# A late query transpose one slot earlier and a weight load one cycle later, in a fused attention and feed-forward kernel

## The chip, the cores and the metric

The kernel runs on one core of a Trainium2 chip. The metric is the device time of one execution in microseconds (us), the median of several runs. Five engines work side by side and meet at semaphores: TensorE (PE; its weight loads are shown apart as PEld), VectorE (DVE), ScalarE (ACT), GpSimd (POOL) and SyncE (SP). Each takes its own instructions strictly in program order, so an instruction that waits holds up all that is queued behind it on the same engine.

## What is computed

```python
def _attn_ref(q, k, v, tau):            # batch 8, heads 8, sequence 576, head size 64
    scores = (1.0 / np.sqrt(q.shape[-1])) * np.matmul(q, k.transpose(0, 1, 3, 2))
    thresh = np.max(scores, axis=-1, keepdims=True) - tau
    scores = np.where(scores >= thresh, scores, -1000000000.0)
    scores = scores - np.max(scores, axis=-1, keepdims=True)
    attn = np.exp(scores)
    attn = attn / (np.sum(attn, axis=-1, keepdims=True) + 1e-09)
    return np.matmul(attn, v)

def _moe_ref(x, w_in, w_out):           # x: 4608 x 512, w_in: 512 x 2048, w_out: 2048 x 512
    h = x @ w_in
    g = h * np.clip(h + 3.0, 0.0, 6.0) / 6.0
    return g @ w_out
```

The attention output, with its heads side by side, is the x of the feed-forward part. Only scores within tau (0.02) of the row's maximum take part in a softmax row.

## The kernel before

**Slots.** The work on the scores is cut into 8 x 18 = 144 slots (the list `queue`, lines 180 to 187). A slot is one batch b, one half g of its heads (a "quad" of four heads, number 2b + g), one tile t of 128 query rows, and a pair i of heads; the order within a batch is (g, t) = (0,0), (0,1), (1,0), (1,1), then the rest tile t = 4, and then (0,2), (0,3), (1,2), (1,3), each twice. The rest tile holds query rows 512 to 575 of both quads of a batch at once. Batch 1 has slots 18 to 35: slots 22 and 23 are tile 0 and slots 24 and 25 tile 1 of quad 3, and slots 26 and 27 are the rest tile of quads 2 and 3.

**What a slot goes through.** `burst(n)` (L216) computes on TensorE the raw scores of slots n and n + 1 into PSUM. Even slots have one place there and odd slots another, so a burst writes over the scores of the two slots before, in steps: part of the even slot, part of the odd slot, and then the rest. `sm_max` (L230) on VectorE copies a slot's scores to SBUF and takes their row maxima, two instructions and two reads of the accumulator; `sm_bias` (L239) on GpSimd makes the threshold from them; `sm_mask` (L244) and `sm_exp` (L249) on ScalarE reject and exponentiate; `sm_recip` (L252) on VectorE inverts the sums; `sm_norm` (L257) on GpSimd normalises and rounds. The result is transposed, on TensorE for slots below 10 (L277, copied by VectorE in L278 and L279), otherwise by a DMA that SyncE issues (L268), and is later multiplied with v (`av`, L286, copied in L294). The feed-forward part runs in between: `mm1` and `mm2_part` (both through L309), a relu (ScalarE L327 in odd slots, VectorE L329 in even ones), a gate (VectorE L342) and an eviction of the output (L361).

**Order.** The order on each engine is that of the program; nothing is rescheduled. There are two loops. The first (line 477) takes slots 0 to 13 in cycles of two; in a cycle n it issues, in one place, the entries `issues[n]` and `issues[n + 1]`, between the maxima of slots n + 2 and n + 3 (only cycle 0 splits them). The second (line 529) takes slots 14 to 143 one by one. In slot n of it stand, in this order: the maxima of slot n + 1 (in odd slots below 21, those of slot n + 2 further down), the reciprocal of slot n - 1, an attention product with its copy, at most one item of the first product with its gate, an eviction that was left over, a part of the second product in odd slots, ScalarE's exponentials and masks, the list `jobs[n]`, the normalisation of slot n - 1, in even slots the burst for slots n + 2 and n + 3, and `issues[n]`. Slots 22, 23 and 24 have no item of the first product.

**Jobs.** Queries and keys are loaded in their natural layout (`load`, L86) and brought into the layout for the scores by block transposes of 32 x 32 on VectorE: `transpose_k` (L110) in two parts, and `transpose_q` (L96) in two pieces, query columns 0 to 255 and 256 to 575. Lines 414 to 426 say in which slot each of these stands. For batch 1 that is a table of its own: quad 2 has its last piece in slot 22 and quad 3 in slot 24. For the other batches, counted from the first slot of the batch before, the last pieces stand in slots 20 and 22.

**Weights.** `load_w_in(i)` (L136) loads a quarter of w_in, 512 KB, with a conversion to bf16, and `load_w_out(i)` (L140) a quarter of w_out. GpSimd issues both, in its own order of instructions, between its biases and normalisations. Lines 442 to 445 give their slots. Quarter 3 of w_in holds hidden columns 1536 to 2047, which the first product reaches with its seventh item, in slot 20.

**Relays.** In a burst, a no-operation on another engine (SyncE in the first loop, GpSimd in the second) waits for the step before, and the burst's last eight or so matmuls, those to the odd slot's last 128 columns, wait for it (lines 204 to 207).

## Time and profile before

| what | value |
|---|---|
| median of 3 runs | 501.76 us (500.86 to 816.31) |
| the profiled execution | 501.7 us, of which 499.9 us are the span of its instructions |
| busy in the span | PE 484.7, DVE 445.8, ACT 441.6, POOL 294.1 us |
| mean granted TensorE clock | 0.997 |
| maxima, DVE L230 | 288 at 750 ns, 205.0 us busy |
| query transposes, DVE L96 | 33, from 404 to 837 ns |
| scores, PE L216 | 2560 matmuls, 168.6 us busy |
| input weight loads, POOL L136 | 4 issues of 512 KB, 747 to 795 ns each on GpSimd, 5.5 to 13.0 us to landing |

Times in the profile count from the first instruction of the span. "Idle before" is the time that an engine stood still before an instruction, with the engine and line that ended it. Ends of matmuls are modelled. The granted clock is the share of full speed at which TensorE was allowed to run. A line such as `DVE s L230 x4` in the chain of waits names engine, written tile, source line and the number of records.

### The profile page before, as it was taken

How to read it: one execution, taken by the hardware profiler on the slowest of the kernel's cores; microseconds unless marked ns; L12 is line 12 of the kernel's file. 1: busy time of each engine (PE TensorE's matmuls, PEld its weight loads, DVE VectorE, ACT ScalarE, POOL GpSimd, SP SyncE). 2: the span in 40 equal slices, each digit the busy share in tenths (PEclk: the TensorE clock that was granted, in tenths of full speed). 3: DMA queues.
4: the chain of work that ended last, by engine and by line, in shares of the span. 5: the costliest groups of instructions: out<-in, count | busy, mean ns of one | idle time of the engine just before them, and what ended most of it. 6: DMA issues, size and time to landing. Idle time of an engine off the chain costs nothing.

```text
span 499.9 us, 17390 instructions
## 1 busy us (share of the span) xinstructions
PE 484.7 (97%) x6797; PEld 359.5 (72%) x6802; DVE 445.8 (89%) x1154; ACT 441.6 (88%) x949; POOL 294.1 (59%) x537
## 2 busy tenths in 40 slices
PE   8888998999999999999999999999999999999996
PEld 7766765777777776777777776777777776777474
DVE  6999986999999999999999999999999999887243
ACT  3999997999999999999999999999999999999231
POOL 3786784666666666666666666766666565554000
PEclk9999998999999999999999999999999999999999
DMA  7999998997999887997999997998999878766421
GB/s 207 150 252 178 148 181 141 180 163 117 178 178 217 130 186 149 227 158 151 156 209 181 152 168 146 220 176 147 160 187 207 151 129 130 134 123 134 92 65 42
DMA packets 192770, 79.98 MB, mean 160 GB/s; under 512 B 171184, under 2 KB 183984, under 8 KB 192688
## 3 DMA queue, kind: packets, MB, share of 16 engines
q1 hardware_dynamic: 175456, 55.34, 65.0%
q0 software_dynamic: 16896, 23.07, 23.9%
q8 instruction: 53, 0.87, 0.7%
q10 hardware_dynamic: 336, 0.46, 0.3%
q14 instruction: 29, 0.24, 0.2%
HBM read 36.70 MB, written 9.44 MB: 92 GB/s over the span
## 4 chain that ended last, share of the span: by engine, by line
PE 82%; DVE 7%; issue 1%; ACT 1%; DMA 0%; SPq 0%; DVEq 0%
PE ps L309 48%; PE ps L216 27%; PE ps L286 7%; DVE s L230 4%; DVE g L342 1%; ACT r L327 1%; DVE osb L361 1%; DMA out_dram<-osb 0%; DVE kT L110 0%; DVE r L329 0%; DVE xT L294 0%; DVE pR L279 0%; SPq L376 0%; DVE qT L96 0%; DVE rinv L252 0%
## 5 line engine op out<-in xcount | busy, mean ns | idle before, releaser
L230 DVE TENSOR_SCALAR_CACHE_REDUCE s<-ps 128x576 f32<-128x576 f32 x288 | 205.0, 750 | 17.9 <-PE ps L216 15.2
L257 POOL TENSOR_SCALAR pn<-s,rinv 128x576 bf16<-128x576 f32 x288 | 210.8, 745 | 14.9 <-issue 1.3
L244 ACT ACTIVATE s<-s,bias 128x576 f32<-128x576 f32 x288 | 205.7, 762 | 8.3 <-POOL bias L239 8.3
L249 ACT ACTIVATE s<-s 128x576 f32<-128x576 f32 x288 | 192.3, 671 | 0.0
L216 PE MATMUL ps<-kT,qT 32*128 32x128 f32 (+3 forms) x2560 | 168.6, 418 | 6.5 <-DVE s L230 4.0
L216 PEld LDWEIGHTS ps<-kT,qT 32*128 32x128 f32 (+1 forms) x2560 | 125.1, 175 | 50.9 <-DVE s L230 11.5
L309 PE MATMUL ps<-xT,w_in_sb 128*64 128x256 bf16 (+1 forms) x1936 | 133.4, 275 | 0.5 <-DVE xT L294 0.5
L309 PE MATMUL ps<-w_out_sb,g 128*64 128x512 bf16 (+1 forms) x1020 | 130.8, 379 | 0.2
L309 PEld LDWEIGHTS <-w_in_sb 128*64 128x64 bf16 (+1 forms) x1936 | 106.0, 109 | 10.9 <-issue 3.3
L239 POOL TENSOR_SCALAR bias<-m 128x2 f32<-128x2 f32 (+1 forms) x147 | 27.6, 188 | 140.1 <-DVE rinv L252 125.9
L342 DVE SCALAR_TENSOR_TENSOR g<-r,ps 128x512 bf16<-128x512 f32 x128 | 87.4, 684 | 12.2 <-ACT r L327 8.5
L309 PEld LDWEIGHTS <-g 128*64 128x64 bf16 (+1 forms) x1024 | 61.6, 109 | 47.9 <-issue 0.2
L327 ACT ACTIVATE r<-ps,three 128x512 f32<-128x512 f32 x81 | 55.2, 686 | 22.8 <-PE ps L309 21.8
L249 ACT ACTIVATION_READ_ACCUMULATOR s<-s 128x1 f32 x288 | 54.6, 190 | 0.0
L286 PEld LDWEIGHTS <-v 128*64 128x64 bf16 x960 | 41.4, 111 | 15.8 <-issue 3.8
L286 PE MATMUL ps<-pT,v 128*64 128x256 bf16 x640 | 45.4, 273 | 1.3 <-DVE s L230 1.2
L329 DVE TENSOR_SCALAR r<-ps 128x512 f32<-128x512 f32 x63 | 43.3, 688 | 0.7 <-PE ps L309 0.4
L119 POOL DMA_DIRECT2D v<-in_v_dram x64 | 36.9, 578 | 10.1 <-DVE kT L110 4.7
L361 DVE TENSOR_SCALAR osb<-ps 128x512 f32<-128x512 f32 x32 | 21.9, 684 | 9.0 <-DMA out_dram<-osb 6.3
L110 DVE STREAM_TRANSPOSE kT<-nk 128x320 f32<-128x320 f32 (+1 forms) x64 | 26.3, 452 | 0.8 <-DMA nk<-in_k_dram 0.8
L294 DVE CAST xT<-ps 128x256 bf16<-128x256 f32 x64 | 26.0, 406 | 0.4
L96 DVE STREAM_TRANSPOSE qT<-nq 128x640 f32<-128x640 f32 (+2 forms) x33 | 24.6, 749 | 1.5 <-DMA nq<-in_q_dram 1.5
(35 smaller groups left out, 170.8 us busy)
## 6 DMA issues: line engine op xcount, KB each, us to landing
out_dram<-osb SPq DMA_DIRECT2D x140, 64.0 KB, 2.6
nk<-in_k_dram POOLq DMA_DIRECT2D x12, 576.0 KB, 4.9
nq<-in_q_dram POOLq DMA_DIRECT2D x12, 576.0 KB, 5.1
v<-in_v_dram POOLq DMA_DIRECT2D x32, 80.0 KB, 4.3
v<-in_v_dram POOLq DMA_DIRECT2D x32, 64.0 KB, 3.4
w_in_sb<-in_moe_w_in_dram POOLq DMA_DIRECT2D x4, 512.0 KB, 7.7
w_out_sb<-in_moe_w_out_dram POOLq DMA_DIRECT2D x4, 512.0 KB, 9.1
pT<-pn SPq DMA_TRANSPOSE x120, 4.5
```

What stands on the lines that cost most here:

```text
L119: nc.gpsimd.dma_start(out=vsb[b % 2][32 * g:32 * g + 32].rearrange("p (hp a) c -> p a hp c", a=2)[:, a, :, c0 * D:(c0 + count) * D], in_=v ...
L216: mm = nc.tensor.matmul(ps_flat[rows, c0:c0 + w], qT[c:c + 32, j, q0:q0 + rows.stop - rows.start], kT[c:c + 32, j, k0:k0 + w], start=(j == ...
L230: nc.vector.tensor_scalar(out=sl.s[:, i, :], in0=ps_flat[:, c0:c0 + S], scalar1=1.0, scalar2=None, op0=Alu.mult, op1=Alu.max, accum_out=sl ...
L239: nc.gpsimd.tensor_scalar(out=sl.bias[:, of], in0=sl.m[:, of], scalar1=-scale, scalar2=tau, op0=Alu.mult, op1=Alu.add)
L244: nc.scalar.activation(out=s, in_=s, func=Act.Prelu, bias=sl.bias[:, i:i + 1], scale=scale, alpha=REJECT)
L249: nc.scalar.activation(out=s, in_=s, func=Act.Exp, accum_out=sl.rsum[:, i:i + 1])
L257: nc.gpsimd.tensor_scalar(out=pn[:, i, :], in0=sl.s[:, i, :], scalar1=sl.rinv[:, i:i + 1], scalar2=1.0, op0=Alu.mult, op1=Alu.mult)
L286: nc.tensor.matmul(pb[a * 64:(a + 1) * 64, :], vsb[b % 2][:, 2 * hp + a, u * D:(u + 1) * D], pT[:, block, cols], start=(c == 0), stop=(c = ...
L309: nc.tensor.matmul(out[c:c + w], lhsT[:, c:c + w], rhs, start=start, stop=stop)
L327: nc.scalar.activation(out=r, in_=hps, func=Act.Relu, bias=three[:])
L329: nc.vector.tensor_scalar(out=r, in0=hps, scalar1=3.0, scalar2=0.0, op0=Alu.add, op1=Alu.max)
L342: nc.vector.scalar_tensor_tensor(out=out, in0=r, scalar=6.0, in1=hps, op0=Alu.min, op1=Alu.mult)
```

## The change

```diff
-        when = (((4, 8, 10, 22), (12, 14, 18, 24)) if b == 1 else ((8, 10, 12, 20), (14, 16, 18, 22)))[g]
+        when = (((4, 8, 10, 22), (12, 14, 18, 23)) if b == 1 else ((8, 10, 12, 20), (14, 16, 18, 22)))[g]
...
-    for i, n in enumerate((0, 2, 2, 3)):
+    for i, n in enumerate((0, 2, 2, 4)):
         at(issues, n, lambda i=i: load_w_in(i))
```

The first edit moves one instruction: `transpose_q(3, 8, T)`, query columns 256 to 575 of quad 3, stands in the jobs of slot 23 and no longer in those of slot 24. The second moves one DMA issue: quarter 3 of w_in is issued in the cycle of slots 4 and 5, between quad 2's query load (on SyncE's queue) and the first quarter of w_out, and no longer in the cycle of slots 2 and 3. No instruction is added or removed.

## The prediction

> **What bounds the kernel now.** I read the page first, then the chain of waits, then the timelines of the single engines around slot 24 and around the weight loads, and last the table by stage for the granted clock. The page says that TensorE is busy 97% of the span and that its granted clock was at nine tenths or more in 39 of 40 slices:

> ```profile
> PEclk9999998999999999999999999999999999999999
> ```

> The one 8 is the seventh slice, about 75 to 87.5 us. The chain of waits (start, duration, what; in us) has a stretch there in which it leaves TensorE for VectorE:

> ```profile
> 77.21 1.34 DVE s L230 x4
> 78.55 0.07 DVE rinv L252
> 78.62 0.32 DVE xT L294
> 78.95 0.60 DVE osb L361
> 79.54 0.76 DVE qT L96
> 80.31 0.04 issue
> 80.35 3.40 PE ps L216 x53
> 83.75 3.15 PE ps L309 x24
> ```

> The reader is to see that the burst of scores (L216) starts when the query transpose (L96) ends. Counted back in program order, this is slot 24. Its VectorE work is the maxima of slot 25 (L230, four records), a reciprocal, the copy of an attention product, an output eviction, and then the job of slot 24, the transpose of quad 3's columns 256 to 575. Right behind it in the program stands the burst for slots 26 and 27, the first that reads those columns: slots 26 and 27 are the rest tile (t = 4, query column 512 on) of quads 2 and 3. TensorE's timeline shows the same from its side, with an ordinary burst above it:

> ```profile
> 72.64 0.48 PE L216 MATMUL ps<-kT,qT 32*128 32x128 f32 x2
> 73.30 2.22 PE L216 MATMUL ps<-kT,qT 32*128 32x128 f32 x30 [0.17 <-DVE s L230]
> ...
> 77.93 0.43 PE L216 MATMUL ps<-kT,qT 32*64 32x128 f32 x2
> ```

> In the ordinary burst the first matmuls run early, and the other 30 start when the second maximum of the odd slot has been read. In slot 24 quad 2's first matmuls run at 77.93, and then TensorE waits 2.00 us for the transpose. The answer on the granted clock by stage (stretch; length; busy PE, PEld, DVE, ACT, POOL; clock; DMA):

> ```profile
> 47.00:50.40 3.40, 2.35 (x68) 1.79 (x68) 3.03 (x13) 3.40 (x9) 1.97 (x5) 1.00 1.26 124
> ...
> 77.90:81.30 3.40, 1.40 (x38) 1.07 (x41) 2.40 (x6) 3.40 (x8) 3.23 (x6) 0.98 0.47 112
> ```

> TensorE was busy 1.40 of 3.40 us here. In steps of half a microsecond, the clock is 1.00 to 81.0, 0.69 in the next step, 0.50 from 81.5 to 84.5, 0.90 to 85.0, and then 1.00 again. Elsewhere the emptiest stretch of 3.4 us that I found still has 2.35 us busy (47.0 to 50.4), and its clock is full. So slot 24 costs a wait and then about 3.3 us at half clock, the only such dip of the run. From 108 us on the chain is almost TensorE alone, so what is won at 80 us should arrive at the end.

> **Part 1, the transpose in slot 23.** Nothing is added or removed: one STREAM_TRANSPOSE of 128x640 (0.83 us by itself, 0.76 of the chain) changes its place on VectorE from behind slot 24's eviction to behind slot 23's reciprocal. Slot 23 has no item of the first product and no copy, so VectorE's order there becomes: maxima of slot 24 (75.69 to 77.05), reciprocal (to 77.13), transpose (to 77.89), and only then the maxima of slot 25, which moves from 77.13 to 77.89. Its data is on the chip long before: quad 3's queries are loaded in slot 9 (issued at 34.03, about 6.7 us to landing).

> What is late next: the transpose no longer ends the wait, but the maxima of slot 25 do, because the burst's second step writes slot 27's scores over slot 25's. They end at 78.54 now and at 78.54 + 0.76 = 79.30 then; in the ordinary burst TensorE follows 0.07 us behind. So the main body starts at 79.37 instead of 80.35: **0.98 us** won. The 0.76 is not won, because the transpose stays ahead of the burst; what is won is the copy (0.32), the eviction (0.60) and the reciprocal (0.07), which now lie behind the release. They wait for nothing there: VectorE idles 3.64 us after 80.29, and their readers on TensorE come after the burst.

> Then the clock. The same burst of 64 matmuls takes 2.20 us at full clock:

> ```profile
> 138.39 2.20 PE L216 MATMUL ps<-kT,qT 32*64 32x128 f32 x64
> ```

> Against 3.40 that is 1.20, and the following group of two products has 3.15 instead of the 2.72 that the chain shows for it from 108 us on, 0.43 more: **1.63 us** for the dip, as 3.3 us at half clock would also give. With the change TensorE's stretch 77.9 to 81.3 holds 0.43 us of first matmuls, and everything from 79.37 to 81.3, at least 2.36 us busy, plus the first matmuls of slot 27. That is as much as the emptiest stretch with full clock, so I take the dip as gone; the bounds are 0 and 1.63.

> [...] The row (2.00 us, then 0.50) decides for me: the drop stands directly behind the run's longest wait of TensorE.

> Other queues that the transpose passes: on GpSimd the bias of slot 25 waits for the later maxima, but it also stands behind a query load that ends at 79.51, and starts at 79.59 today; with maxima at 79.30 it needs no more. ScalarE's mask of slot 25 starts at 80.39, behind ScalarE's own work. GpSimd's two normalisations then run from 79.86 to 81.32, and the relay of the burst (a GpSimd nop that the last eight matmuls wait for) stands behind them: the burst would end at 79.37 + 2.20 = 81.57, so this costs 0 to 0.1 us. After the burst, the maxima of slot 27 must be read before the next burst: VectorE's work between, with ScalarE's in its chain, leaves about 0.5 us to spare if all of it moves up by 2.6.

> **Part 2, the fourth input weight load.** Two slots are one cycle of the first loop: slots 2 and 3 are issued together, so today GpSimd issues three of these loads in one cycle, and the fourth moves to the cycle of slots 4 and 5, ahead of the first output weight load:

> ```profile
> 20.93 2.29 POOL L136 DMA_DIRECT2D w_in_sb<-in_moe_w_in_dram  x3
> 23.29 0.18 POOL L239 TENSOR_SCALAR bias<-m 128x2 f32<-128x2 f32 x1
> ...
> 26.56 0.19 POOL L239 TENSOR_SCALAR bias<-m 128x2 f32<-128x2 f32 x1
> 26.81 0.79 POOL L140 DMA_DIRECT2D w_out_sb<-in_moe_w_out_dram  x1
> 27.69 0.18 POOL L239 TENSOR_SCALAR bias<-m 128x2 f32<-128x2 f32 x1
> ```

> One issue is 2.29 / 3 = 0.76 us. It moves past the bias of slot 5, the normalisations of slots 2 and 3 and the bias of slot 6, all of which come some 0.7 us earlier. Then two loads end at about 26.1 + 0.76 + 0.79 = 27.65, and the bias of slot 7 stands where it was (27.69). Who gains: ScalarE waits 0.45 us for the bias of slot 6 at 26.78, and TensorE's transposes wait 0.17, 0.27 and 0.32 us for the normalised rows. Neither is on the path: ScalarE works ahead of its readers until it waits again, 0.21 us for a bias at 54.34, and the burst at 26.91 must wait for the maxima of slot 7, which VectorE, without a gap since 24.38, ends at 27.10 whatever GpSimd does. So I take 0. Bounds: 0.45 won if ScalarE's wait carried through, 0.79 lost if the two issues stood ahead of the normalisations and these had not moved up; the value lies nearest to the row of 27.69, which does not move. The data itself has cover: landing took at most 13.0 us, so about 39 us, and these columns are first multiplied in slot 20, after 60 us.

> **The sum.** Span 499.9, run 501.7: 1.8 us lie outside, and the median of the runs is 501.76, so one sum serves both. 501.7 - 0.98 - 1.63 - 0 = 499.1.

> **The rivals.** *B: the wait gets shorter, the dip stays.* For it speaks the gate's unknown rule, since TensorE still idles about 0.5 to 1 us in pieces around 78.5; against it, that such pieces occur at 16 us and at 100 us at full clock. 501.7 - 0.98 = 500.7. *C: slower, by the clock gate.* If the gate samples stretches whose place is not tied to the waits, a shift by 1 us can put another ragged stretch, the one between 98 and 107 us with idle pieces of 0.29, 0.41, 0.20 and 0.67 us, under it, while the dip at 81 stays. One dip more costs 1.63: 501.7 - 0.98 + 1.63 = 502.4. It decides from two dips on; with one moved dip the result is B's. *D: the move does nothing,* because the maxima or GpSimd's relay end the burst as late as before. The rows leave 0.98 us between the releases, and for D all of it would have to be lost: 501.7.

> **How the numbers follow.** Forecast 499.1 with 0.74; B 500.7 with 0.13; C 502.4 with 0.06; D 501.7 with 0.07. The forecast's own range takes part 2's bounds in part and 0.1 for the relay: 498.5 to 499.9. For 8 in 10 I take B in as well: 498.4 to 500.9. Two per cent, 10 us, is about what a measurement of this kernel can tell from no change; every case lies within 3 us, so within 2% gets 0.97. Slower gets 0.02, because one of the three runs shown stands at 816.31, and faster 0.01.

> **What would show it.** Right: in TensorE's timeline the wait of 2.00 us for qT is gone and the burst's body follows the maxima of slot 25, near 79.4; the clock stays at 1.00 through 81 to 85; the burst for slots 26 and 27 takes about 2.2 us; GpSimd's rows show two input weight loads and then two loads in the next cycle, with the bias of slot 7 near 27.7; all later rows stand about 2.6 us earlier. Wrong: a half-clock stretch in any slice, a burst body that starts after 80, or rows between 30 and 75 us that have moved by more than 0.3 us, which would make part 2 more than a shuffle.

## The result, and the profile after

The changed kernel took 499.66 us (median of 22 runs, 499.30 to 501.69), the kernel before 502.05 us (22 runs, 500.29 to 506.73 and one of 816.31). The medians are 2.39 us apart. The ratio is 0.9965, with an interval of 0.9951 to 0.9979: 1.75 us faster, between 1.05 and 2.46. It goes with the averages, which are 501.72 and 499.98 us without the two stray times of before (506.73 and 816.31). At 2% such a ratio is no difference, but it is clear of zero. The forecast was 499.1 in a range of 498.4 to 500.9.

The chain of waits of the changed kernel at slots 23 to 25 (start, duration, what; us):

```profile
76.12 1.44 DVE s L230 x4
77.56 0.08 DVE rinv L252
77.64 0.74 DVE qT L96
78.38 1.35 DVE s L230 x4
79.72 0.04 issue
79.77 2.19 PE ps L216 x50
81.96 2.72 PE ps L309 x32
```

The query transpose stands before the second group of maxima, and these now release the burst. The copy (L294) and the eviction (L361) have left the chain. The burst takes 2.19 us instead of 3.40 and the two products behind it 2.72 instead of 3.15. TensorE's timeline and the answer on the granted clock by stage (the columns as before) say the same:

```profile
79.09 0.43 PE L216 MATMUL ps<-kT,qT 32*64 32x128 f32 x4 [0.74 <-DVE s L230]
79.77 2.19 PE L216 MATMUL ps<-kT,qT 32*64 32x128 f32 x60 [0.24 <-DVE s L230]
```

```profile
77.90:81.30 3.40, 2.42 (x56) 1.66 (x56) 2.81 (x8) 3.40 (x9) 3.20 (x6) 1.00 0.42 79
...
81.00:84.00 3.00, 3.00 (x62) 2.10 (x48) 1.81 (x6) 2.25 (x4) 0.96 (x4) 1.00 0.99 246
```

The wait of 2.00 us has become two of 0.74 and 0.24, and the clock stays at 1.00.

All of these rows stand 0.43 us late, and the reader must know why before subtracting: by its letter, the prediction's sign for a part 2 that is more than a shuffle (rows between 30 and 75 us moved by more than 0.3 us) has come. The first query transpose that waits for its load starts at another time in each profile, before and after:

```profile
13.38 0.71 DVE L96 STREAM_TRANSPOSE qT<-nq 128x512 f32<-128x512 f32 x1 [0.46 <-DMA nq<-in_q_dram]
```

```profile
13.81 0.71 DVE L96 STREAM_TRANSPOSE qT<-nq 128x512 f32<-128x512 f32 x1 [0.72 <-DMA nq<-in_q_dram]
```

This row lies ahead of both edits. Over all profiles of this study it moves between 13.34 and 14.21, and kernels without either edit have both ends. I call it the start row and measure later rows from it. One caution: it lies at 13.81 to 14.18 in the six profiles with the transpose moved, and at 13.34 to 13.71 in the others but for the one at 14.21, so these rows alone do not show that the change has no part in it. The times speak against a part: the lower group of before averages 500.58 us and the changed kernel's executions at full clock 499.67, and in a later group of runs it is 500.64 and 499.62. That is 0.91 and 1.02 us, about the 1.01 that the start row leaves for the transpose. The body of the burst starts 80.35 - 13.38 = 66.97 us behind the start row before, and 79.77 - 13.81 = 65.96 after: 1.01 us earlier. The end of the span comes 486.5 and 483.9 us behind it: 2.6 us earlier.

GpSimd's timeline around the weight loads:

```profile
21.35 1.54 POOL L136 DMA_DIRECT2D w_in_sb<-in_moe_w_in_dram  x2
22.97 0.18 POOL L239 TENSOR_SCALAR bias<-m 128x2 f32<-128x2 f32 x1
...
26.41 0.19 POOL L239 TENSOR_SCALAR bias<-m 128x2 f32<-128x2 f32 x1 [0.25 <-DVE s L230]
26.84 0.79 POOL L136 DMA_DIRECT2D w_in_sb<-in_moe_w_in_dram  x1 [0.24 <-issue]
27.63 0.75 POOL L140 DMA_DIRECT2D w_out_sb<-in_moe_w_out_dram  x1
28.46 0.18 POOL L239 TENSOR_SCALAR bias<-m 128x2 f32<-128x2 f32 x1
```

Two loads, then two, as the diff says. The bias of slot 5 comes 0.75 us earlier against the start row and that of slot 6 0.58; that of slot 7 comes 0.34 later (28.46 - 0.43 against 27.69).

### The profile page after: what moved, and what is told of

The parts are those of the page before. It is cut to its first block, busy times and chain, and to the rows that moved or that the text cites. A ratio compares the mean times of both kernels' runs of the same rounds, so it can differ in the third digit from the quotient of the medians.

```text
span 497.7 us, 17390 instructions
## 1 busy us (share of the span) xinstructions
PE 483.0 (97%) x6797; PEld 358.4 (72%) x6802; DVE 445.7 (90%) x1154; ACT 441.8 (89%) x949; POOL 294.1 (59%) x537
## 4 chain that ended last, share of the span: by engine, by line
PE 82%; DVE 6%; issue 1%; ACT 1%; DMA 0%; SPq 0%; DVEq 0%
PE ps L309 48%; PE ps L216 27%; PE ps L286 7%; DVE s L230 4%; DVE g L342 1%; ACT r L327 1%; DVE osb L361 0%; DMA out_dram<-osb 0%; DVE kT L110 0%; DVE r L329 0%; DVE pR L279 0%; SPq L376 0%; DVE xT L294 0%; DVE qT L96 0%; DVE rinv L252 0%
## 5 line engine op out<-in xcount | busy, mean ns | idle before, releaser
L230 DVE TENSOR_SCALAR_CACHE_REDUCE s<-ps 128x576 f32<-128x576 f32 x288 | 204.9, 749 | 15.8 <-PE ps L216 13.0
L216 PE MATMUL ps<-kT,qT 32*128 32x128 f32 (+3 forms) x2560 | 167.5, 414 | 6.5 <-DVE s L230 5.9
L216 PEld LDWEIGHTS ps<-kT,qT 32*128 32x128 f32 (+1 forms) x2560 | 124.3, 174 | 50.8 <-DVE s L230 14.0
L309 PE MATMUL ps<-xT,w_in_sb 128*64 128x256 bf16 (+1 forms) x1936 | 133.0, 274 | 0.5 <-DVE xT L294 0.5
L309 PE MATMUL ps<-w_out_sb,g 128*64 128x512 bf16 (+1 forms) x1020 | 130.8, 379 | 0.2
L309 PEld LDWEIGHTS <-w_in_sb 128*64 128x64 bf16 (+1 forms) x1936 | 105.7, 109 | 10.6 <-issue 3.1
L239 POOL TENSOR_SCALAR bias<-m 128x2 f32<-128x2 f32 (+1 forms) x147 | 27.6, 188 | 137.7 <-DVE rinv L252 123.4
L309 PEld LDWEIGHTS <-g 128*64 128x64 bf16 (+1 forms) x1024 | 61.6, 109 | 47.9 <-issue 0.2
L361 DVE TENSOR_SCALAR osb<-ps 128x512 f32<-128x512 f32 x32 | 21.8, 682 | 9.0 <-DMA out_dram<-osb 6.3
L294 DVE CAST xT<-ps 128x256 bf16<-128x256 f32 x64 | 25.9, 405 | 0.4
L96 DVE STREAM_TRANSPOSE qT<-nq 128x640 f32<-128x640 f32 (+2 forms) x33 | 24.6, 748 | 1.9 <-DMA nq<-in_q_dram 1.9
```

The lines of the kernel that those rows point to most:

```text
L216: mm = nc.tensor.matmul(ps_flat[rows, c0:c0 + w], qT[c:c + 32, j, q0:q0 + rows.stop - rows.start], kT[c:c + 32, j, k0:k0 + w], start=(j == ...
L230: nc.vector.tensor_scalar(out=sl.s[:, i, :], in0=ps_flat[:, c0:c0 + S], scalar1=1.0, scalar2=None, op0=Alu.mult, op1=Alu.max, accum_out=sl ...
L239: nc.gpsimd.tensor_scalar(out=sl.bias[:, of], in0=sl.m[:, of], scalar1=-scale, scalar2=tau, op0=Alu.mult, op1=Alu.add)
L309: nc.tensor.matmul(out[c:c + w], lhsT[:, c:c + w], rhs, start=start, stop=stop)
```

## The experiments

The question left by the result: the profiles differ by 2.6 us, the measured times by 1.75. And before's 22 times are not one heap: 7 lie from 500.29 to 500.86, the others from 501.76 up. My theory was that the half-clock stretch behind the wait comes in some executions only. The rivals: the moved load takes part of the gain back, or the stretch has nothing to do with the wait. The mean granted clock of each execution, at the end of this section, tells the two groups apart.

**Each edit alone, and the transpose one slot earlier still.**

```diff
# e1_transpose_alone
-        ... (12, 14, 18, 24)) if b == 1 ...
+        ... (12, 14, 18, 23)) if b == 1 ...
# e2_load_alone
-    for i, n in enumerate((0, 2, 2, 3)):
+    for i, n in enumerate((0, 2, 2, 4)):
# e3_slot22
-        ... (12, 14, 18, 24)) if b == 1 ...
+        ... (12, 14, 18, 22)) if b == 1 ...
```

> Only the transpose in slot 23; the weight load as before. Theory: all of the gain is the transpose's. The burst body starts 0.98 us earlier than before (against its own start of the run), the 22 times of before fall into two groups (500.3 to 500.9 and 501.8 to 502.9) because the half-clock stretch of 1.63 us comes in some executions only, and the changed place makes it rarer. So this kernel is 1.5 to 2.5 us faster than before, as the whole change is (ratio 0.995 to 0.997). Rival: the moved load holds part of the gain or of a loss; then this kernel differs from the whole change by 0.4 us or more.

> Only the fourth weight load one cycle later; the transpose in slot 24 as before. Theory: no effect, ratio 1.000 within 0.001, times in the same two groups as before, the wait of 2.00 us for the transpose in TensorE's timeline. Rival: the bias of slot 7, some 0.3 us later after the change, costs 0.3 to 0.8 us; ratio 1.0006 to 1.0016, and the rows after 30 us stand later against the rows at 15 us.

> The transpose in slot 22, behind quad 2's, the load as before. Theory: it fits into the 1.30 us in which VectorE waits for the burst of slot 22, so it moves nothing, the maxima of slot 25 end as before the change, and the burst body starts another 0.76 us earlier than with slot 23. 1.7 us for the wait and most of the half-clock stretch: 2.3 to 3.3 us faster than before (ratio 0.9935 to 0.9955). Rival: VectorE is the bound there whatever the order, and the time is that of slot 23.

The transpose alone: 499.64 us, ratio 0.9952 (0.9936 to 0.9968), the body 65.96 us behind the start row; the whole change has 499.66 and 65.96. The load alone: 502.04 us, ratio 0.999 (0.9975 to 1.0005), times in both groups, the body 66.96 behind the start row, as before. Its GpSimd rows repeat the 0.3 us at the bias of slot 7, and nothing later has moved. The interval alone would leave room for 1.3 us won or 0.3 lost; it is the rows that show the load to be a shuffle that nobody waits for. Neither rival came: the medians of the transpose alone and of the whole change agree to 0.02 us, and the load alone is not slower.

In slot 22: 499.18 us, ratio 0.9948 (0.9928 to 0.9968). TensorE's timeline of this kernel, whose start row is at 14.06:

```profile
78.59 0.43 PE L216 MATMUL ps<-kT,qT 32*64 32x128 f32 x4
79.27 2.19 PE L216 MATMUL ps<-kT,qT 32*64 32x128 f32 x60 [0.24 <-DVE s L230]
```

The first matmuls wait for nothing, and the body starts 65.21 us behind the start row, 0.75 earlier than with slot 23. So the transpose does fit into the 1.30 us in which VectorE waits for the burst of slot 22. The expectation named the place to 0.01 us. Two of its six times, 500.52 and 500.98, have a mean granted clock of 0.997 where the others have 0.999 to 1.000; what that means is said below.

**The wait filled, with nothing moved.**

```diff
# e4_filled_wait: before, and
+        if n == 24:
+            for _ in range(16):
+                nc.tensor.transpose(ps[:, HB, 0:P], identf[:], identf[:])
         if n % 2 == 0 and n + 2 < len(queue):
             burst(n + 2)
# e10_half_filled: the same with range(8)
```

> Before, with 16 identity transposes more on TensorE in slot 24 (into a PSUM bank that nobody reads until slot 25), ahead of the burst: the wait for the query transpose stays, but TensorE is busy through it. Theory: the clock falls because TensorE idles; so the burst body starts where it did before, the clock is 1.00 throughout, the burst takes 2.2 us, and all times lie in the lower group (500.3 to 500.9; ratio about 0.998). [...]

The result is 500.88 us, ratio 0.9974 (0.996 to 0.9988); ten of twelve times lie between 500.29 and 501.58, the other two at 510.24 and 513.0. TensorE's timeline, start row at 14.21:

```profile
78.69 1.97 PE L574 MATMUL ps<-identf 128*128 128x128 f32 x16
80.58 0.43 PE L216 MATMUL ps<-kT,qT 32*64 32x128 f32 x2
81.19 2.19 PE L216 MATMUL ps<-kT,qT 32*64 32x128 f32 x62 [0.18 <-DVE qT L96]
```

The body starts 66.98 us behind the start row, no earlier than before, yet the burst takes 2.19 us. The only thing taken away here is TensorE's idleness, so the stretch at 81 us comes from it. The upper group is nearly gone: by the mean granted clock of each execution (0.998 to 1.000, against 0.997 and less) it is 3 of 12, the time of 501.58 and the two high ones, against 15 of the 23 runs of before beside it.

**The wait made longer.**

```diff
# e5_doubled: before, and after the jobs of a slot
+        if n == 24:
+            transpose_q(3, 8, T)
```

> Before, with the query transpose of slot 24 done twice (the same values written again), so that TensorE's wait there is 0.76 us longer, 2.76 us. Theory: the body starts 0.76 us later, and the half-clock stretch, which the upper group of before's times has and the lower has not, comes in every execution: all times near 502.2 + 0.8 = 503.0, a ratio of 1.002 to 1.004, and the lower group is gone. Rival: the stretch comes by chance whatever the wait is; two groups remain, each 0.8 us higher (501.4 and 503.0).

The result is 503.52 us, ratio 1.0041 (1.0023 to 1.0059). The wait is 2.88 us. In the profiled execution (503.85 us) the clock is 0.50 from about 80.3 to 87.1, twice as long as before:

```profile
81.40 4.14 PE L216 MATMUL ps<-kT,qT 32*64 32x128 f32 x62 [2.88 <-DVE qT L96]
85.47 1.82 PE L309 MATMUL ps<-xT,w_in_sb 128*64 128x256 bf16 x16
```

But not "in every execution": 3 of 12 times lie at 501.13 to 501.51, which is where before's lower group with 0.8 us more would be. On this part the rival was nearer: even with 2.88 us the stretch comes by chance, only more often and, in some executions, longer: of the nine others five have a mean granted clock of 0.997, as one stretch of 3.4 us gives, and four 0.991 to 0.993, as two or a little more give.

**What is left in the changed kernel.** The changed kernel with 10 fillers, the changed kernel once more, and with the transpose in slot 22:

```diff
# e6_after_filled: after, and ahead of burst(n + 2) in slot 24
+            for _ in range(10):
+                nc.tensor.transpose(ps[:, HB, 0:P], identf[:], identf[:])
# e7_after_again: after, unchanged
# e9_slot22_with_load
-        ... (12, 14, 18, 23)) if b == 1 ...
+        ... (12, 14, 18, 22)) if b == 1 ...
```

> The changed kernel with 10 identity transposes on TensorE in slot 24 ahead of the burst, in its remaining idle time of about 1 us. They end near the release, so the body starts within 0.2 us of where it did. Theory: the few times of the changed kernel near 501 (4 of 22) are executions with a half-clock stretch here; with the filling none is left, and the median stays at 499.6 to 499.9. Rival: those few have another cause and stay.

> The changed kernel itself, on the chip of the others of this group. Theory: median 499.5 to 499.8, about one time in five near 501; rows from 20 to 75 us that stand against before by the same amount as those at 15 us, since what is later there comes from the load of the first queries.

> The changed kernel with the transpose in slot 22. Theory: as with the transpose in slot 22 and the old place of the load: body at the end of slot 25's maxima, 0.76 us earlier than the changed kernel, of which about 0.5 is left at the end: median 499.0 to 499.3, and hardly any time above 500.5, since TensorE's idle time in slot 24 is below 0.5 us. Rival: above-500.5 times as often as in the changed kernel, so they do not come from slot 24.

Filled: 499.92 us, ratio 1.000 (0.997 to 1.0031), and 5 of 12 times above 500.5 (500.95, 501.21 and three at 505.69 to 507.62). The expectation that none would be left fell, and the rival held: all five have a mean granted clock of 0.995 to 0.997, so they were throttled although slot 24 was filled. The changed kernel again: 499.73 us, ratio 0.9971 (0.9958 to 0.9983), all 9 times from 499.31 to 499.83, so that 4 of its 31 times in all lie at 501.01 to 501.69. Those four have a mean granted clock of 0.996 to 0.997 and the other 27 one of 0.998 to 1.000, so each had about one half-clock stretch. Where it lay stays open, as no profile fell on one. Kernels with slot 24 filled, or with only 0.24 us of idle time there (the two high times with slot 22), have it too, so slot 24 is not the only place. Seven times of the three fillings are stray, 2 to 12 us higher. The unchanged kernel has a few such times too (505.77 and 506.73), and their cause was not looked into; idle-time fillers are therefore no cure to recommend from this.

Slot 22 with the load: 499.08 us, six times from 498.33 to 500.11, ratio 0.9958 (0.9942 to 0.9975) against runs of before that fell low in this group of runs. Against the changed kernel on the same chip it is 499.08 to 499.73. No kernel of the study has a lower median. The body starts 65.22 us behind the start row, and the span ends 0.67 us earlier against the start row than the changed kernel's.

**Half filled, and before again.**

> Before, with 8 identity transposes in place of 16 in slot 24, so that about 1 us of TensorE's wait of 2 us stays idle. Theory: what decides is how much idle time falls into one sampling stretch; 1 us left is as much as the changed kernel has, so the half-clock stretch is gone as with the full filling: all times near 500.8, the upper group (501.7 and more) gone, ratio 0.997 to 1.000 depending on how many of before's own runs fall high. Rival: the gate looks for any gap; then the upper group remains.

The result is 500.64 us, ratio 0.9984 (0.9961 to 1.0007); ten of twelve times from 500.05 to 500.83, two higher (502.29 and 504.02). All twelve have a mean granted clock of 0.998 to 1.000, the two higher ones 1.000 and 0.999, so those two are late for another reason. With 1.05 us of idle time left, the body 66.97 us behind the start row, and the burst at 2.19 us, the profile shows no stretch at 81 us.

> Before once more, for its spread and for another profile. Theory: the times fall into the same two groups, about 1.5 us apart; if the profiled execution is of the lower group its clock is 1.00 through 78 to 86 us although TensorE waits 2.00 us all the same, and if it is of the upper one it has a half-clock stretch of about 3.3 us behind the wait. Rival: a profile of the lower group shows the stretch too, or one of the upper lacks it; then the groups come from elsewhere.

> Before a third time, for one more profile; expected as the run before it: lower time without, higher time with the half-clock stretch at 81 us.

> Before a fourth time, for a profile of an execution of the lower group, which has not been seen yet. Theory: a time near 500.6 goes with a clock of 1.00 from 78 to 86 us behind the same wait of 2.00 us, a time near 502.2 with a half-clock stretch there. Rival: a low time with the stretch, or a high one without.

The first of these runs has a median of 502.42 us (12 times, ratio 1.0007, 0.9983 to 1.0032). The first two profiles fell on 501.93 and 501.96 us and showed the stretch; the third, on another chip, fell on 500.33. The last two side by side, the one at 501.96 us first (TensorE's timeline, then clock by stage):

```profile
80.60 3.85 PE L216 MATMUL ps<-kT,qT 32*64 32x128 f32 x62 [2.00 <-DVE qT L96]
84.38 1.06 PE L309 MATMUL ps<-xT,w_in_sb 128*64 128x256 bf16 x16
```

```profile
81.00:84.00 3.00, 3.00 (x55) 2.31 (x42) 0.00 (x0) 1.05 (x2) 0.57 (x1) 0.50 1.08 252
```

and the one at 500.33 us:

```profile
80.59 2.19 PE L216 MATMUL ps<-kT,qT 32*64 32x128 f32 x62 [2.00 <-DVE qT L96]
82.72 1.06 PE L309 MATMUL ps<-xT,w_in_sb 128*64 128x256 bf16 x16
```

```profile
81.00:84.00 3.00, 3.00 (x78) 2.38 (x63) 0.99 (x3) 1.23 (x3) 0.57 (x1) 1.00 1.04 236
```

It is the same program with the same start row (13.63 in both), and the same wait to the hundredth. One execution has the half clock, the other has not, and they differ by 1.63 us in time and 1.6 in span. This is the difference between the two groups.

The mean granted clock, which is recorded for every execution and not only for the profiled one, says the same of all. 3.4 us at half clock take 0.0034 off the mean of 500 us. The runs of before beside the experiments have 71 such times, without one of 1695.06: all 34 up to 501.20 us have 1.000, and all 37 from 501.60 have 0.993 to 0.997. Four of these, at 503.63 to 504.78, have 0.993, as two stretches give, and lie on average 3.4 us above the lower group.

## Why the prediction was right, and where it was not

- *The release.* Predicted: the body starts 0.98 us earlier, at the end of slot 25's maxima. Measured: 1.01, in the changed kernel and with the transpose alone, with the release where it was named. The relay on GpSimd cost nothing that shows: the burst took 2.19 us.
- *The load.* Predicted 0. Measured: its kernel alone has a ratio of 0.999 with 1 inside the interval and no shifted row behind it. One detail was off: the bias of slot 7 was to stand still, and came 0.34 us later, because the bias of slot 6 waits for its maxima and the two loads start behind it. Nobody waited for that.
- *The dip, the mis-sized term.* The mechanism was right, and 1.63 us was the right price: the two profiles of before differ by just that. But the sum took it off in full, as if every execution of before had it. In the 22 runs that the change was measured against, 14 times lie in the upper group and 7 in the lower, without the one of 816.31. So its mean worth there is about 14 / 21 x 1.63 = 1.1 us, and 0.98 + 1.1 = 2.1 us, less what the changed kernel's own four high times take back (4 / 22 x 1.5 = 0.3): 1.8 against the measured 1.75. The median shows more, 2.39 of the forecast 2.6, because more than half of before's times carry the stretch. That is luck of the group of runs: in the one with only 8 of 25 in the upper group the medians are 500.81 and 499.73, 1.08 us apart. The profile that I worked from had fallen on the commoner case, and the 500.86 among the three times shown was the hint that I passed over.
- *The rule that was unknown.* A gap of 2.00 us was followed by half the clock in four profiles and not in a fifth; in the four it began 0.84, 0.38, 0.28 and 0.12 us behind the end of the wait and lasted 3.41 us, and with a wait of 2.88 us 6.83. So the row (2.00 us, then 0.50) was rightly read as a wait and what came of it, but not as something that every execution has. The differing distances agree with the grid of 3.413 us in the traces.
- *The rivals.* B (the dip stays) and C (a dip elsewhere) show in no profile of the changed kernel, but by the mean granted clock 4 of its 31 executions had about one half-clock stretch, so in about one of eight something of their kind came, at an unknown place. C's condition, stretches whose place is not tied to the waits, is what the grid shows. D (nothing moves) did not come.
- *The absolute time.* 499.1 was forecast and 499.66 measured. The profiled execution took 499.51, and its start row is 0.43 us later than that of the profile I took as base, which is about the difference (13.38 there; in the two later profiles of before with the half clock 13.51 and 13.63). From the start row to the end the forecast was 486.5 - 2.6 = 483.9, and so it is. The median is another 0.15 above the profiled execution.

## What to carry to other kernels

When a job on an in-order engine releases another engine, list what stands ahead of it and ask whether that must; then ask which release is late next, for only the difference is won. Look for a slot in which the engine waits anyway, and put the job there, ahead of the instruction that waits: with slot 22 the burst's body started 1.75 us earlier than before, with slot 23 1.01. And before pricing something that a profile shows once, look whether the times of the runs form groups: a cost that comes by chance is worth, on average, its price times its share, and the granted clock of each execution tells which ones paid it (for before, beside the experiments, 0.993 to 0.997 against 1.000).

## What the runs showed that I had not expected

- A single wait of 2.00 us of TensorE was enough, in 51 of 92 times of the unchanged kernel (the runs of before beside the change and the experiments, without two stray ones above 800 us, cut at 501.4), to put it among the times that go with about 3.4 us or more at half clock. With 1.05 us of idle time it was none of 12 by the mean granted clock, with 2.88 us 9 of 12.
- That share differs between groups of runs of one kernel: 14 of 21, 15 of 23, 8 of 25 and 14 of 23, and 10 of 12 in the run of it as an experiment. A comparison of two kernels is therefore uncertain by some tenths of a microsecond on that ground alone.
- The start-up shifted whole executions by up to 0.87 us (the start row, 13.34 to 14.21), nearly as much as the 1.01 us that the moved transpose won.
